# A transformer block on one Trainium2 core: the order of VectorE's work in the attention loop, the bank of two maxima a unit, and the place of one q/k set

## The chip, the core and the metric

The kernel runs on one core of one Trainium2 chip. TensorE (PE) multiplies, VectorE (DVE) and ScalarE (ACT) work on the sums in PSUM and on data in SBUF, GpSimd (POOL) on data in SBUF, and SyncE (SP) issues all DMAs here. The metric is the device time of one execution in microseconds; a lower one is better.

## The reference

Input x has 2048 tokens of 640 values. With xn = layernorm(x) the output is

```
q, k, v = split(xn @ wqkv)                 # 32 heads of 20 values
s = q k^T / sqrt(20), masked to 0 <= i - j < 256
attention = softmax(s) v @ wo
mlp = (gelu(xn @ w_gate) * (xn @ w_up)) @ w_down    # 1728 wide, gelu by tanh
out = x + attention + mlp
```

All is float32. The kernel gets the accuracy by splitting each float32 operand of the large products into a high and a low part and adding three products (high by high, low by high, high by low).

## The kernel before, in words

**Stages.** First a prologue: layernorm, transposes of x into its high and low parts `xh` and `xl`, and the first projections. Then the attention loop (`attention`, L705), which also computes most of the q, k and v projections and the first gate/up tiles of the MLP as fill. Then the other gate/up tiles (L825), and last the product with w_down and wo (L1276). The change lies in the attention loop.

**The loop.** Heads are taken in 8 groups of four and tokens in 4 chunks of 512, which makes 32 units `u = (g, c)`. A unit has 14 slots (`NS`). In each slot the program first emits the deferred work that is due (`tick`, L697), then, in even slots, two score pieces (`exp_piece`, L479: matmuls into the PSUM tile `ps_e`, L493, and an Exp on ScalarE into `P`, L495) and two or three maximum pieces, and last some 3 matmuls of fill (`pull_fill`, L700). In slot 0 it also emits the products P times V of the unit before (`av_unit`, L507: `ps_o`, L515, copied out by ScalarE into `ob`, L519), and in slot 11 the DMA loads of the q and k stacks of the unit three ahead (`load_stack`, L413, L421). A ramp of 12 slots ahead of unit 0 runs 24 maximum pieces, so the maxima run one and a half units ahead of the score pieces.

**Maxima.** The softmax needs a maximum for each row of scores. `max_piece` (L427) lets TensorE compute a 128-row strip of scores into the PSUM tile `ps_m` (L441), from a pool of three buffers (`psm`), and VectorE takes its maximum under the mask (L443, shown in the trace as the instruction itself and a short read of the accumulator `mx`). A unit has 16 of them: two in each even slot, three in slots 6 and 12. After the sixteenth, VectorE writes the negated maxima in two short instructions (L448, L449), four slots later TensorE transposes them (`max_end`, L452: `ps_n`, L455, in the same pool), ScalarE copies them to `mr` (L457) and a DMA puts them beside q in `qs` (L458), where the score pieces of that unit read them.

**Fill.** The generator `filler` (L594) yields groups of 15 matmuls with 512 columns into `ps_d` (L100, a pool of two buffers), about five slots for each group. What has to be done with a group's sum is deferred by slots with `defer` (L194):

- a q/k group (`save_qk`, L216): one slot later ScalarE copies the high part (`pt`, L235) and VectorE subtracts it (`r`, L236), one slot after that ScalarE copies the middle part (L223), POOL makes the low part (L224) and SP stores the three (L230). `r` has one buffer, `pt` two.
- a gate group and an up group (`gate_up_fill`, L550): ScalarE copies and squares (L558, L559), a slot later VectorE (L564), a slot later ScalarE's Tanh (L568), a slot later VectorE (L572), and when the up group is there VectorE multiplies (L579) and SP stores (L580).

The fill goes by the list `sets` (L589): each q/k set projects one 128-row tile of q and one of k for all four chunks, each gate/up set one tile of the MLP. The v projection of the second half of the heads (`V1_SLOT`) comes in at the first end of a chunk from slot 158 on. A stack load needs the q/k tiles of its heads in DRAM: units 24 and later need the fourth set.

**What sets the order.** On TensorE, VectorE and ScalarE the loop's instructions run in the order in which the program emits them (`manual_schedule`, L744). POOL's and SP's orders are made by the scheduler of the framework. Each engine runs its own instructions in order, so a waiting one holds all behind it. In the pages, SPq, DVEq and so on are an engine's sequencer. POOL also works in the background on sums of x (`x_sums`, L631: `tx`, L642, stored to `td`, L645), on the causal edges of `P` (L501, L504) and on the low parts of weights (L545).

Of the kernel before, what the change touches and what calls it, by code (L numbers as in the profile page):

```python
# [9 lines left out]
F32 = mybir.dt.float32  # L10
# [3 lines left out]
OP = mybir.AluOpType  # L14
# [10 lines left out]
NF = 14  # L25
# [8 lines left out]
NFA = 6  # L34
# [26 lines left out]
def block_kernel(ctx, tc, x, wqk, wv, wgu, wdo, wdl, out):  # L61
    nc = tc.nc
# [66 lines left out]
    psm = pp.enter_context(tc.tile_pool(name="psm", bufs=3, space=PSUM))  # L129
    pso = pp.enter_context(tc.tile_pool(name="pso", bufs=1, space=PSUM))  # L130
# [56 lines left out]
    acts = {}  # L187
    done = set()
    now = [None]

    def at(slot, fn, *a):
        acts.setdefault(slot, []).append((fn, a))

    def defer(n, fn, *a):  # L194
        if now[0] is None:
            fn(*a)
        else:
            at(now[0] + n, fn, *a)
# [17 lines left out]
    def save_qk(t, c, ps):  # L216
        pt = qkp.tile([128, 3, C], BF, name="pt", tag="pt")
        r = qkp.tile([128, C], F32, name="r", tag="r", bufs=1)
        dst = (qd if t < 5 else kd)[c]
        h, l = (2, 0) if t < 5 else (0, 2)  # L220

        def lower():
            nc.scalar.activation(pt[:, 1, :], r, AF.Copy)  # L223
            nc.gpsimd.tensor_tensor(out=pt[:, l, :], in0=r, in1=pt[:, 1, :], op=OP.subtract)  # L224
            a, end = t % 5 * 128, t % 5 * 128 + 128
            while a < end:
                g, b = divmod(a, 4 * DH)
                n = min(4 * DH - b, end - a)
                p = n - end + a + 128
                nc.sync.dma_start(dst[g, :, b:b + n, :].rearrange("p m t -> m p t"), pt[p - n:p])  # L230
                a += n
            done.add((t, c))

        def upper():
            nc.scalar.activation(pt[:, h, :], ps, AF.Copy)  # L235
            nc.vector.tensor_tensor(out=r, in0=ps, in1=pt[:, h, :], op=OP.subtract)  # L236
            defer(1, lower)

        defer(1, upper)

# [52 lines left out]
    def run(*gens):  # L293
        for gen in gens:
            for _ in gen:
                pass
# [84 lines left out]
    with tc.tile_pool(name="lp", bufs=1, side="right") as lp:  # L381
# [3 lines left out]
        ps = psd.tile([128, C], F32, name="ps_u", tag="dn")  # L385
# [38 lines left out]

    maxes = {}

    def max_piece(u, i):  # L427
        g, c = divmod(u, NC)
        j, b = divmod(i, 4)
        q, k = qs[u % NQ], ks[u % NK]  # L430
        if i == 0:
            maxes[u] = ap.tile([128, 4, 4], F32, name="mx", tag="mx")
        ps = psm.tile([128, 384], F32, name="ps_m", tag="mx")
        lh = q[0:120, j, 128 * b:128 * b + 128]
        old = max(0, 256 - 128 * b) if c else 0
        n0 = max(0, 128 * b - 256)
        n = old + 128 * b + 128 - n0
        parts = [(0, old, ks[(u - 1) % NK][0:120, j, C - old:C])] if old else []
        parts.append((old, n, k[0:120, j, n0:128 * b + 128]))
        for lo, hi, rhs in sorted(parts, key=lambda p: p[1] - p[0]):  # L440
            nc.tensor.matmul(ps[:, lo:hi], lh, rhs, start=True, stop=True)  # L441
        junk = ap.tile([128, 384], BF, name="junk", tag="junk", bufs=1)
        nc.vector.tensor_tensor_reduce(out=junk[:, 0:n], in0=ps[:, 0:n], in1=mask[:, 384 - n:384], scale=1.0,  # L443
                                       scalar=NEG, op0=OP.add, op1=OP.max, accum_out=maxes[u][:, j, b:b + 1])
        if i == 15:
            mx = maxes.pop(u)
            nm = nms[u % 2]
            nc.vector.tensor_scalar(nm[:, 0, 0], mx, -1.0, None, op0=OP.mult)  # L448
            nc.vector.scalar_tensor_tensor(nm[:, 0, 1], mx, -1.0, nm[:, 0, 0], op0=OP.mult, op1=OP.subtract)  # L449
            maxes[u] = nm  # L450

    def max_end(u):  # L452
        nm = maxes.pop(u)
        ps = psm.tile([128, 128], F32, name="ps_n", tag="mx")
        nc.tensor.matmul(ps, nm.rearrange("p z a j b -> p (z a j b)"), identb, start=True, stop=True)  # L455
        mr = ap.tile([32, 128], BF, name="mr", tag="mr")
        nc.scalar.activation(mr, ps[0:32], AF.Copy)  # L457
        nc.sync.dma_start(qs[u % NQ][120:122].rearrange("p j t -> p (j t)"), mr)  # L458
# [91 lines left out]
    def gate_up_fill(f, ws, c):  # L550
        cs = slice(c * C, (c + 1) * C)
        pss = []
        st = {}

        def c1():
            gs = st["g"] = hp.tile([128, C], F32, name="gs", tag="gs")
            t = st["t"] = hp.tile([128, C], F32, name="he", tag="he", bufs=2)
            nc.scalar.activation(gs, pss[0], AF.Copy)  # L558
            nc.scalar.activation(t, pss[0], AF.Square, scale=math.sqrt(0.044715))  # L559
            defer(1, c2)  # L560

        def c2():
            gs, t = st["g"], st["t"]
            nc.vector.scalar_tensor_tensor(t, t, 1.0, gs, op0=OP.add, op1=OP.mult)  # L564
            defer(1, c3)

        def c3():
            nc.scalar.activation(st["t"], st["t"], AF.Tanh, scale=math.sqrt(2.0 / math.pi))  # L568
            defer(1, c4)

        def c4():
            nc.vector.scalar_tensor_tensor(st["g"], st["t"], 1.0, st["g"], op0=OP.add, op1=OP.mult)  # L572
            st["done"] = True

        def c5():
            if "done" not in st:
                defer(1, c5)
                return
            nc.vector.scalar_tensor_tensor(st["t"], st["g"], 0.5, pss[1], op0=OP.mult, op1=OP.mult)  # L579
            nc.sync.dma_start(hd[f][c], st["t"])  # L580

        for i, (wh, wl) in enumerate(ws):
            ps = psd.tile([128, C], F32, name="ps_d", tag="dn")
            pss.append(ps)
            yield from dense_steps(ps, lambda k: wh[:, k, :], lambda k: wl[:, k, :],
                                   lambda k: xh[:, k, cs], lambda k: xl[:, k, cs], KT)
            defer(1, c5 if i else c1)

    sets = [("qk", 1), ("gu", 0), ("qk", 2), ("qk", 3), ("gu", 1), ("qk", 4)]  # L589
    sets += [("gu", f) for f in range(2, NFA)] + [("gu", NF - 1)]  # L590
    pools = (wp, None), (hp, 2)
    rest = []

# [91 lines left out]
    fill = filler()  # L685
    debt = [0.0]

    def pull_max(n, slot):
        for _ in range(n):
            x = next(stream, None)  # L690
            if x is None:
                return
            max_piece(*x)
            if x[1] == 15:
                at(slot + MXD, max_end, x[0])

    def tick():  # L697
        return [y for t in sorted(t for t in acts if t <= now[0]) for y in acts.pop(t)]

    def pull_fill(n):  # L700
        debt[0] += n
        while debt[0] > 0:
            debt[0] -= next(fill, 1.0)

    def attention():  # L705
        now[0] = -1
        load_stack(0)
        load_stack(1)
        load_stack(2)
        for i, (p, k, half) in enumerate((p, k, half) for p in range(NC // 2) for k in range(2) for half in range(2)):  # L710
            for j, fn in enumerate(x_sums(p, k, half)):
                at(XS0 + XSN * i + 2 * j, fn)
        for i in range(12):
            now[0] = i - 13
            for fn, a in tick():
                fn(*a)
            for _ in range(2):
                pull_max(1, now[0])
                pull_fill(RAMP)
        pull_fill(GAP)  # L720
        for u in range(NU + 1):
            for i in range(NS):
                T = now[0] = NS * u + i
                for fn, a in tick():
                    fn(*a)
                if i == 0 and u:
                    av_unit(u - 1)
                if i % 2 == 0:
                    if u < NU and i < 12:
                        exp_piece(u, i)  # L730
                        exp_piece(u, i + 1)
                    pull_max(3 if i in (6, 12) else 2, T)
                if i == 11 and 3 <= u + 3 < NU:
                    load_stack(u + 3)
                pull_fill(RATE / NS)
        while acts:
            now[0] += 1
            for fn, a in tick():
                fn(*a)
        now[0] = None  # L740
        run(fill)
        assert not acts
# [9 lines left out]
    c2 = c2s.enter_context(tc.tile_pool(name="c2", bufs=1, reuse_waits="tile"))  # L752
# [501 lines left out]
    late = list(tasks)[2:]  # L1254
# [21 lines left out]
    for n, (p, k) in enumerate(steps):  # L1276
        i = n % (NQD + 1)
        if i == 0:
            begun.clear()
            ps = {b: psn.tile([128, C], F32, name=f"ps_{b}", tag=f"b{b}") for b in (1, 2, 5, 3, 6, 4, 7, 8)}  # L1280
# [59 lines left out]
```

## Time and profile before

| | us |
|---|---|
| median of 3 runs | 1093.71 |
| lowest and highest | 1092.64, 1094.08 |
| the profiled execution, its own time | 1093.39 |
| its span, first to last instruction | 1091.7 |
| prologue and ramp, about | 0 to 93 |
| attention loop, about | 93 to 657 |
| other gate/up tiles, about | 657 to 835 |
| product with w_down and wo, about | 835 to 1092 |

The profiled execution takes 1.69 us beside its span. The granted TensorE clock is 0.998 of full speed over the span. A group row of the profile gives the line, the engine, the operation, the tiles (out<-in), the shape and the count, then the busy time and the mean duration in ns, then the idle time of the engine just before these instructions and what ended it. A row of waits gives the total, the number and the longest. A row of the chain gives start, length and what ran. In a timeline row the bracket is the idle time before the instruction and what ended it.

### The profile page before, as it was taken

The numbers are of one execution on the slowest core, as the hardware profiler recorded it, in microseconds if no ns is written. First come the engines' busy times: TensorE is split into PE (matmuls) and PEld (weight loads), VectorE is DVE, ScalarE is ACT, GpSimd is POOL, SyncE is SP. The second block draws the span as 40 slices with busy tenths as digits, with TensorE's granted clock in tenths as the row PEclk, the third lists the DMA queues.
The fourth block names the chain that finished last, engine by engine and source line by source line (L and its number), as shares of the span: only waits on it lengthen the run. The fifth ranks groups of instructions, "written<-read, shape, count | busy, mean of one in ns | idle before, by whom it ended". The sixth has DMA issues, their size and how long they took to land.

```text
span 1091.7 us, 20910 instructions
## 1 busy us (share of the span) xinstructions
PE 1073.2 (98%) x7253; PEld 857.9 (79%) x7253; DVE 757.4 (69%) x2089; ACT 509.7 (47%) x1031; POOL 335.3 (31%) x513
## 2 busy tenths in 40 slices
PE   8999999999999999999999999999999999999998
PEld 7887666666678766666766678888888899999998
DVE  7756667565666575666766636788875579888886
ACT  4434655465645556455555464323234453333332
POOL 5045634566726444645335240111110000000000
PEclk9999999999999999999999999999999999999999
DMA  5642343446442333353332325588764885343433
GB/s 206 195 137 82 114 143 91 132 126 181 141 135 69 87 114 112 117 163 111 103 113 83 100 62 194 178 271 286 265 210 150 293 283 166 110 141 112 138 121 114
DMA packets 96057, 162.30 MB, mean 149 GB/s; under 512 B 13248, under 2 KB 57920, under 8 KB 95952
## 3 DMA queue, kind: packets, MB, share of 16 engines
q1 hardware_dynamic: 95952, 160.97, 46.8%
q8 instruction: 57, 0.93, 0.4%
q14 instruction: 48, 0.39, 0.1%
HBM read 104.40 MB, written 56.23 MB: 147 GB/s over the span
## 4 chain that ended last, share of the span: by engine, by line
PE 78%; DVE 9%; DMA 5%; ACT 3%; issue 3%; SPq 1%; POOL 1%; DVEq 0%; ACTq 0%
PE ps_d L100 23%; PE ps_g L843 15%; PE ps L1087 12%; PE ps_o L515 7%; PE ps_e L493 7%; PE ps_m L441 6%; PE ps_v L100 6%; DVE ss L933 2%; DMA hr<-hd 1%; PE ps_g L100 1%; DVE junk L443 1%; DMA stg<-wdo 1%; DVE xr L1101 1%; ACT at L1047 1%; ACT P L495 1%
## 5 line engine op out<-in xcount | busy, mean ns | idle before, releaser
L443 DVE CUSTOM_DVE_ANT_0 junk<-ps_m,mask 128x384 bf16<-128x384 f32 (+2 forms) x512 | 271.6, 531 | 177.5 <-PE ps_m L441 136.3
L495 ACT ACTIVATE P<-ps_e 128x512 f32<-128x512 f32 (+2 forms) x384 | 197.7, 568 | 63.7 <-PE ps_e L493 57.6
L1087 PE MATMUL ps<-wb,at 128*128 128x320 f32 x999 | 159.1, 312 | 0.6 <-DVE wb L933 0.3
L1087 PEld LDWEIGHTS ps<-wb,at 128*128 128x128 f32 x999 | 150.2, 189 | 2.8 <-DVE wb L933 1.1
L501 POOL TENSOR_SCALAR_AFFINE_SELECT P<-P 128x512 f32<-128x512 f32 x128 | 84.1, 657 | 176.1 <-ACT P L495 169.1
L100 PE MATMUL ps_d<-xh,wql 128*128 128x512 f32 x430 | 129.3, 410 | 0.0
L100 PE MATMUL ps_d<-xl,wqh 128*128 128x512 f32 x430 | 128.5, 408 | 0.0
L100 PE MATMUL ps_d<-xh,wqh 128*128 128x512 f32 x430 | 128.5, 409 | 0.0
L441 PE MATMUL ps_m<-ks,qs 120*128 120x128 bf16 (+1 forms) x704 | 120.9, 275 | 3.8 <-DVE mx L443 2.0
L493 PE MATMUL ps_e<-qs,ks 122*128 122x128 bf16 (+2 forms) x704 | 113.1, 277 | 1.5 <-ACT P L495 0.8
L493 PEld LDWEIGHTS <-ks 122*128 122x128 bf16 x704 | 50.2, 98 | 55.1 <-issue 44.5
L1087 PE MATMUL ps<-wt,at 128*128 128x320 f32 x552 | 89.9, 310 | 1.2 <-DVE u L933 1.1
L100 PEld LDWEIGHTS ps_d<-xh,wql 128*128 128x128 f32 x430 | 77.9, 189 | 15.8 <-issue 2.3
L100 PEld LDWEIGHTS ps_d<-xl,wqh 128*128 128x128 f32 x430 | 78.3, 188 | 14.8 <-issue 0.6
L100 PEld LDWEIGHTS ps_d<-xh,wqh 128*128 128x128 f32 x430 | 77.7, 189 | 14.1 <-ACT xh L184 0.3
L441 PEld LDWEIGHTS <-qs 120*128 120x128 bf16 x704 | 62.1, 98 | 32.9 <-issue 14.1
L1087 PEld LDWEIGHTS ps<-wt,at 128*128 128x128 f32 x552 | 83.0, 188 | 2.3 <-DVE u L933 1.6
L515 PE MATMUL ps_o<-P,v 128*32 128x384 f32 (+2 forms) x1408 | 84.3, 386 | 0.0
L504 POOL TENSOR_SCALAR_AFFINE_SELECT P<-P 128x512 f32<-128x512 f32 x112 | 72.6, 659 | 37.4 <-ACT P L495 37.4
L224 POOL TENSOR_TENSOR pt<-r,pt 128x512 bf16<-128x512 f32 x40 | 46.8, 1170 | 79.7 <-ACT pt L223 79.6
L515 PEld LDWEIGHTS ps_o<-P,v 128*32 128x32 f32 x1408 | 40.1, 110 | 39.5 <-issue 29.2
L1047 ACT ACTIVATE at<-ss 128x512 fp32r<-128x512 f32 x59 | 37.2, 630 | 71.5 <-DVE ss L933 71.1
(179 smaller groups left out, 1696.7 us busy)
## 6 DMA issues: line engine op xcount, KB each, us to landing
hr<-hd SPq DMA_DIRECT2D x104, 128.0 KB
hd<-he SPq DMA_DIRECT2D x50, 256.0 KB
wr<-wgu SPq DMA_DIRECT2D x27, 320.0 KB
qs<-qd SPq DMA_DIRECT2D x32, 240.0 KB
ks<-kd SPq DMA_DIRECT2D x32, 240.0 KB
ats<-wdo SPq DMA_DIRECT2D x9, 640.0 KB
wtd<-ats SPq DMA_DIRECT2D x9, 640.0 KB
stg<-wtd SPq DMA_DIRECT2D x9, 640.0 KB
```

What stands on the lines that cost most here:

```text
L100: nc.tensor.matmul(ps, a(k), b(k), start=n == 0, stop=n == 3 * nk - 1)
L224: nc.gpsimd.tensor_tensor(out=pt[:, l, :], in0=r, in1=pt[:, 1, :], op=OP.subtract)
L441: nc.tensor.matmul(ps[:, lo:hi], lh, rhs, start=True, stop=True)
L443: nc.vector.tensor_tensor_reduce(out=junk[:, 0:n], in0=ps[:, 0:n], in1=mask[:, 384 - n:384], scale=1.0, scalar=NEG, op0=OP.add, op1=OP.max ...
L493: nc.tensor.matmul(ps[:, col:col + n], k[0:QROWS, j, kc:kc + 128], q[0:QROWS, j, q0:q0 + n], start=True, stop=True)
L495: nc.scalar.activation(pt[:, j, lo:hi], ps[:, lo:hi], AF.Exp, scale=SCALE)
L501: nc.gpsimd.affine_select(out=a, in_=a, pattern=[[0, 4], [1, 128]], compare_op=OP.is_ge, fill=0.0, base=0, channel_multiplier=-1)
L504: nc.gpsimd.affine_select(out=a, in_=a, pattern=[[0, 4], [-1, 128]], compare_op=OP.is_ge, fill=0.0, base=-1, channel_multiplier=1)
L515: nc.tensor.matmul(o[32 * j:32 * j + 32, q0:q0 + n], v[:, w0_:w0_ + 32], pt[:, j, col:col + n], start=i == 0, stop=i == len(todo) - 1, ski ...
L843: nc.tensor.matmul(ps, i, j, start=first and n == 0, stop=n == len(work) - 1, skip_group_check=True)
L1047: nc.scalar.activation(hi[:, 3:7], s, AF.Copy)
L1087: nc.tensor.matmul(ps[bank][:, 0:HD], a, b, start=bank not in begun, stop=final[p, bank] == n and j == len(work[bank]) - 1, skip_group_che ...
```

## The change

Three things are changed, all in the emission of the attention loop.

- **Late work.** A list `lates` takes VectorE work that is called with `late`; `flush` emits it at the end of each slot, after the slot's maxima and ahead of its fill. The subtract of a q/k group, the gate/up steps `c2`, `c4` and `c5`, and the two negations of the maxima go through it. What follows the subtract (`lower`) and what follows `c2` (`c3`) is deferred by two slots in place of one. `tick` emits `max_end` after the other deferred work of the slot.
- **Bank.** The second maximum of slot 6 and the first of slot 10 take a tile of the pool `pso`, the one bank in which `ps_o` lies, in place of one of `psm`. These are 61 of the 512 maxima.
- **Order of the fill.** In `sets` the fourth q/k set stands ahead of gate/up tile 1 instead of behind it.

No instruction is added or removed on any engine, and TensorE's instructions stand in the same order as before but for the two sets, whose matmuls have the same shapes.

```
+    lates = []
+
+    def late(fn, *a):
+        if now[0] is None:
+            fn(*a)
+        else:
+            lates.append((fn, a))
+
+    def flush():
+        while lates:
+            fn, a = lates.pop(0)
+            fn(*a)
...
+        def middle():
+            nc.vector.tensor_tensor(out=r, in0=ps, in1=pt[:, h, :], op=OP.subtract)
+            defer(2, lower)
+
         def upper():
             nc.scalar.activation(pt[:, h, :], ps, AF.Copy)
-            nc.vector.tensor_tensor(out=r, in0=ps, in1=pt[:, h, :], op=OP.subtract)
-            defer(1, lower)
+            late(middle)
...
-    def max_piece(u, i):
+    def max_piece(u, i, where):
...
-        ps = psm.tile([128, 384], F32, name="ps_m", tag="mx")
+        pool, tag = where
+        ps = pool.tile([128, 384], F32, name="ps_m", tag=tag)
...
-            nc.vector.tensor_scalar(nm[:, 0, 0], mx, -1.0, None, op0=OP.mult)
-            nc.vector.scalar_tensor_tensor(nm[:, 0, 1], mx, -1.0, nm[:, 0, 0], op0=OP.mult, op1=OP.subtract)
             maxes[u] = nm
+
+            def negate():
+                nc.vector.tensor_scalar(nm[:, 0, 0], mx, -1.0, None, op0=OP.mult)
+                nc.vector.scalar_tensor_tensor(nm[:, 0, 1], mx, -1.0, nm[:, 0, 0], op0=OP.mult, op1=OP.subtract)
+
+            late(negate)
...
-            defer(1, c2)
+            defer(1, late, c2)
...
-            defer(1, c3)
+            defer(2, c3)
...
-            defer(1, c4)
+            defer(1, late, c4)
...
-                defer(1, c5)
+                defer(1, late, c5)
...
-            defer(1, c5 if i else c1)
+            defer(1, *((late, c5) if i else (c1,)))
-
-    sets = [("qk", 1), ("gu", 0), ("qk", 2), ("qk", 3), ("gu", 1), ("qk", 4)]
-    sets += [("gu", f) for f in range(2, NFA)] + [("gu", NF - 1)]
+
+    sets = [("qk", 1), ("gu", 0), ("qk", 2), ("qk", 3), ("qk", 4)]
+    sets += [("gu", f) for f in range(1, NFA)] + [("gu", NF - 1)]
...
-    def pull_max(n, slot):
-        for _ in range(n):
+    def pull_max(n, slot, other=None):
+        for k in range(n):
...
-            max_piece(*x)
+            max_piece(*x, (pso, "o") if k == other else (psm, "mx"))
...
     def tick():
-        return [y for t in sorted(t for t in acts if t <= now[0]) for y in acts.pop(t)]
+        todo = [y for t in sorted(t for t in acts if t <= now[0]) for y in acts.pop(t)]
+        return sorted(todo, key=lambda y: y[0] is max_end)
...
                 pull_max(1, now[0])
+                flush()
                 pull_fill(RAMP)
...
-                    pull_max(3 if i in (6, 12) else 2, T)
+                    pull_max(3 if i in (6, 12) else 2, T, {6: 1, 10: 0}.get(i))
+                flush()
                 if i == 11 and 3 <= u + 3 < NU:
                     load_stack(u + 3)
                 pull_fill(RATE / NS)
...
             for fn, a in tick():
                 fn(*a)
+            flush()
```

## The prediction on record

> **What bounds the kernel now.** I read the page's busy line first, then the table by stretches for the attention loop, then TensorE's groups in that stretch.
>
> ```profile
> PE 1073.2 (98%) x7253; PEld 857.9 (79%) x7253; DVE 757.4 (69%) x2089; ACT 509.7 (47%) x1031; POOL 335.3 (31%) x513
> 93.00:657.00 564.00, 558.52 (x4256) 391.16 (x4254) 355.20 (x1175) 310.09 (x642) 286.19 (x453) 1.00 0.38 114
> L441 PE MATMUL ps_m<-ks,qs 120*128 120x384 bf16 (+2 forms) x672 | 113.0, 275 | 3.8 <-DVE mx L443 2.0 <-DMA sd<-ob 1.5
> L493 PE MATMUL ps_e<-qs,ks 122*128 122x256 bf16 (+2 forms) x702 | 112.6, 277 | 1.5 <-ACT P L495 0.8
> ```
>
> TensorE bounds the loop: busy 558.52 of 564.00 us, with VectorE at 355.20 and ScalarE at 310.09. The change gives TensorE the same matmuls in the same order, so all it can win in the loop is TensorE's waiting. The visible part is 564.00 - 558.52 = 5.48 us, nearly all of it ahead of the maxima (3.8) and the score pieces (1.5). As the ends of matmuls are modelled, a short wait can hide under the matmul before, so this is a low figure. A better one comes from the lengths of the units. Each unit begins with the products P times V, so the starts of `ps_o` in the chain that ended last mark the units (the x32 rows are unit 1 and every fourth after it; they follow a first chunk, which has fewer pieces).
>
> ```profile
> 106.12 2.08 PE ps_o L515 x32
> ...
> 285.49 2.73 PE ps_o L515 x48
> 303.04 2.73 PE ps_o L515 x48
> ...
> 373.51 2.73 PE ps_o L515 x48
> 390.90 2.08 PE ps_o L515 x32
> 408.22 2.73 PE ps_o L515 x48
> 425.87 2.73 PE ps_o L515 x48
> 443.66 2.77 PE ps_o L515 x48
> 480.74 2.73 PE ps_o L515 x48
> ...
> 622.77 2.73 PE ps_o L515 x48
> ```
>
> Units 1 to 29 take 622.77 - 106.12 = 516.65 us, 17.82 each, or 17.82 / 14 = 1.27 a slot. A good unit of each chunk: unit 16 takes 390.90 - 373.51 = 17.39, unit 17 takes 17.32, unit 18 takes 17.65, unit 11 takes 303.04 - 285.49 = 17.55, together 69.91. Seven such fours and one more unit like 17 make 7 x 69.91 + 17.32 = 506.69. So about **10.0 us** of the loop is irregular waiting, and the change can win that and little more.
>
> What these waits are is seen in timelines. First VectorE and then TensorE in unit 1, slots 10 to 12:
>
> ```profile
> 118.04 0.56 DVE L443 CUSTOM_DVE_ANT_0 junk<-ps_m,mask 128x384 bf16<-128x384 f32 x1
> ...
> 118.75 0.56 DVE L443 CUSTOM_DVE_ANT_0 junk<-ps_m,mask 128x384 bf16<-128x384 f32 x1
> ...
> 120.21 0.69 DVE L236 TENSOR_TENSOR r<-ps_d,pt 128x512 f32<-128x512 f32 x1 [0.89 <-ACT pt L235]
> 120.81 0.55 DVE L443 CUSTOM_DVE_ANT_0 junk<-ps_m,mask 128x384 bf16<-128x384 f32 x1
> ```
>
> ```profile
> 122.48 0.32 PE L441 MATMUL ps_m<-ks,qs 120*128 120x384 bf16 x1 [0.65 <-DVE mx L443]
> ```
>
> The subtract stands ahead of the slot's maxima and waits 0.89 us for ScalarE's copy; the maxima wait behind it, their buffers stay full, and TensorE stands 0.65 us. A maximum takes 118.75 - 118.04 = 0.71 us with its readout. Second, ScalarE in unit 9, and its waits for VectorE over the loop:
>
> ```profile
> 255.34 0.60 ACT L235 ACTIVATE pt<-ps_d 128x512 bf16<-128x512 f32 x1
> 256.76 0.63 ACT L223 ACTIVATE pt<-r 128x512 bf16<-128x512 f32 x1 [0.83 <-DVE r L236]
> 257.30 2.14 ACT L495 ACTIVATE P<-ps_e 128x512 f32<-128x512 f32 x4
> ```
>
> ```profile
> ACT he L568 <- DVE he L564: 15.1, 13, 2.2
> ...
> ACT pt L223 <- DVE r L236: 13.8, 18, 1.9
> ```
>
> With one slot between the subtract and the copy that needs it, ScalarE reaches the copy too early and stands (13 + 18 times), and then does four Exps in a row: the score pieces behind find their two buffers full. Third, SyncE and TensorE in units 20 and 21:
>
> ```profile
> 451.75 7.11 SPq L645 DMA_DIRECT2D td<-tx  x2
> ...
> 464.20 0.78 SPq L230 DMA_DIRECT2D kd<-pt  x2
> 465.07 1.37 SPq L421 DMA_DIRECT2D qs<-qd  x3
> 466.49 1.10 SPq L421 DMA_DIRECT2D ks<-kd  x3
> ```
>
> ```profile
> 472.73 0.33 PE L441 MATMUL ps_m<-ks,qs 120*128 120x128 bf16 x2 [1.50 <-DMA sd<-ob]
> ```
>
> SP holds at a store of `tx`, then at the last store of the fourth q/k set (`kd`); only then come the stack loads of unit 23, and TensorE waits 1.50 us for them at its first maximum of that unit. Units 20 and 21 together take 480.74 - 443.66 = 37.08, against 17.39 + 17.32 = 34.71 for their kind.
>
> **The change part by part.** No instruction comes or goes, so every term is a wait.
>
> *Late work.* The waits other than the one of the stack are 10.0 - 1.5 = 8.5 us; they come from VectorE's order and from ScalarE waiting for VectorE. With the maxima first, the subtract's wait for ScalarE lies beside 2 x 0.71 = 1.42 us of maxima, more than the 0.89 seen. Its own end moves back: in a slot with two maxima it ends 1.42 + 0.69 = 2.11 us after the first maximum begins, in one with three 3 x 0.71 + 0.69 = 2.82. What needs it now comes two slots later, 2 x 1.27 = 2.54. So in six of seven slots (all but slots 6 and 12) ScalarE finds it done, in the others it waits some 0.3 us. The negations, 0.53 us for the second one, go behind the third maximum of slot 6 too:
>
> ```profile
> L449 DVE SCALAR_TENSOR_TENSOR nm<-mx,nm 128x16 bf16<-128x16 f32 x31 | 16.5, 533 | 1.1
> ```
>
> Behind the late work stand only the next even slot's maxima, which start two slots later anyway. `ps_d` is kept some 1.4 us longer; its buffer is next wanted a whole group (five slots, 6.3 us) later, so this costs nothing, and without that cover up to 1.4 a group. The sum of one unit of 16 x 0.71 = 11.4 us of maxima and about three groups' late work of 0.7 to 2.1 fits in 17.4. Of the 8.5 us I take four fifths, **-6.8**: below it is nothing (the waits only change place), above it all 8.5.
>
> *Bank.* 61 of the 512 maxima get a fourth buffer. The one of slot 6 waits for ScalarE's copy of `ps_o`, issued in slot 0; that of slot 10 must be read before `ps_o` is written again, four slots or 5.1 us later, against 0.71. Nothing waits there. Alone it gains where a slot with three maxima meets a late VectorE, which is in the 8.5 already: 0 here. If VectorE were late by more than four slots, P times V would stand, by as much.
>
> *Order of the fill.* The fourth set's 120 matmuls, its eight sums with their copies, subtracts and POOL parts, its 16 stores, its two loads and its splits move ahead of gate/up tile 1's 120 matmuls, ScalarE and VectorE steps, four stores and two loads; on SP and POOL they change places with these. TensorE's sum is the same. At the time of the stack of unit 23 SP then has no `kd` store in front of it and POOL no low part of a set, so the 1.50 us go: **-1.5**, bounded by 0 (the `tx` store still stands ahead) and -2.4 (37.08 - 34.71). What was at that place now falls some three units earlier, on other stacks, which is in the next term.
>
> *New waits.* ScalarE still meets slots with three maxima, stores come a slot later, and `mr` is emitted behind the slot's other ScalarE work. I take **+0.5**, between 0 and the rivals below.
>
> *A rule of the Trainium skill.* VectorE's two steps with both inputs in SBUF now lie elsewhere beside POOL's work:
>
> ```profile
> L564 DVE SCALAR_TENSOR_TENSOR he<-he,gs x24: 685/691/1169, 148.8 to 652.0; 128x512 f32<-128x512 f32 x24
> L572 DVE SCALAR_TENSOR_TENSOR gs<-he,gs x24: 679/687/1089, 150.6 to 653.5; 128x512 f32<-128x512 f32 x24
> ```
>
> A few take 0.4 to 0.48 us more than the median. The Trainium skill (SBUF — State Buffer, section Who interferes with whom) says why: a VectorE instruction with two SBUF inputs and a GpSimd one that reads SBUF exclude each other for a whole instruction. The long ones in these rows agree. By that rule alone the loss is that of the third rival.
>
> **Sum.** -6.8 - 1.5 + 0.5 = -7.8. The profiled execution's own time is 1093.39 (span 1091.7 and 1.69 around it): 1093.39 - 7.8 = **1085.6 us**, 0.74% under the median 1093.71, which lies 0.3 above the profiled execution. With all of the 10.0 and 0.4 of unit 0 it would be 1083.0. The stages after the loop follow it at a fixed distance.
>
> **The rivals.**
>
> 1. *Half comes back.* In slots with three maxima, or where ScalarE runs late, the late step still misses its user. Half of the 6.8 stays, and SP finds the stack of unit 23 late as before: -3.4 + 0.5 = -2.9, 1090.5 us. For it: 31 waits of ScalarE are to be cured by one more slot, and VectorE's part moves back by up to three maxima (2.1 us), more than that slot (1.27). Against it: six of seven slots have room.
> 2. *Slower: SP's queue.* SP already stands at stores whose data is not ready:
>
> ```profile
> SPq L580 <- DVE he L579: 71.3, 17, 8.5
> SPq L230 <- POOL pt L224: 68.8, 25, 5.5
> ```
>
>    Both kinds become ready later (by up to 2.1 us and by 1.27), and stack loads and `mr` queue behind. The rows of the copy, of its DMA's issue, and of a small store from issue to landing in the chain:
>
> ```profile
> L457 ACT ACTIVATE mr<-ps_n x32: 250/268/268, 85.8 to 636.2; 32x128 bf16<-32x128 f32 x32
> ```
>
> ```profile
> L458 SPq DMA_DIRECT2D qs<-mr x32: 632/667/712, 86.1 to 636.7; - x32
> ```
>
> ```profile
> 591.89 1.71 DMA sd<-ob
> ```
>
>    `mr` leaves TensorE in slot 10 and is needed in slot 14, 5.1 us later; less 0.27 for the copy, 0.67 for the issue and, as an estimate from the store, 1.7 for landing, 2.4 are free. Where SP is held longer than that, TensorE waits. If eight of the units lost 1.5 us each, as unit 21 does now, that is +12.0 - 6.8 + 0.5 = +5.7: 1099.1 us. Against it: the profile shows one such wait in 31 units.
> 3. *Same: POOL and VectorE in each other's way.* If all 48 of the steps above took 0.45 more, one in a slot with three maxima would end 2.13 + 1.15 = 3.28 us after the first, 0.7 beyond the two slots. At 0.15 us of TensorE for each that is 7.2, and the gain is gone: 1085.6 + 7.2 = 1092.8. The medians, at the lowest value, speak against it.
>
> That the change does not do what it says is hardly possible: VectorE's order is written out by hand.
>
> **How the numbers follow.** Forecast (1083.0 to 1088.5): 0.60. Half comes back (1088.5 to 1091.5): 0.18. No change (1091.5 to 1095.9): 0.10, half of it the third rival and half waits that only change their place. SP's queue, slower than 1095.9: 0.09. Better than 1083.0: 0.03. A measurement of this kernel can tell 0.2% (2.2 us) from no change, which gives faster 0.60 + 0.18 + 0.03 = 0.81, same 0.10, slower 0.09. The range 1083.0 to 1092.0 leaves out 0.03, 0.09 and most of the 0.10, about 0.2.
>
> **What would show it.** Late work: TensorE's idle time ahead of the maxima falls from 3.8 us to under 1, ScalarE's waits of 15.1 and 13.8 to a third, and units 1 to 29 take some 509 us. Order of the fill: no stand of TensorE at the first maximum of unit 23. Wrong would be: idle time ahead of the score pieces above 1.5 us, with SP held at a store just before; a wait of P times V for a maximum; or units that keep their 17.8 us.

## The result and the profile after

The changed kernel takes **1096.7 us** (median of 8 runs, 1093.79 to 1099.39), the kernel before in the same series 1093.89 (8 runs, 1091.78 to 1095.58). The ratio is 1.0026 with a 95% interval of 1.0014 to 1.0039: slower by about 2.8 us, where the prediction said 8 us faster. The profiled execution of the changed kernel took 1098.06 us, 4.67 more than that of the kernel before (1093.39), so part of what follows is larger in it than in the median.

The line numbers move: L441, L443, L493, L515 of the kernel before are L458, L460, L514, L536 after; the subtract L236 is L248, the copies L235 and L223 are L252 and L236, POOL's L224 is L237, the store of `mr` L458 is L479, the stores of `pt` and `tx` L230 and L645 are L243 and L666. The split of the weights in the ramp is L92 in both.

First TensorE's groups of the kernel after from 93 to 662 us, the loop, as they were shown of before:

```profile
L458 PE MATMUL ps_m<-ks,qs 120*128 120x384 bf16 (+2 forms) x676 | 113.3, 275 | 1.1 <-DVE mx L460 0.7
L514 PE MATMUL ps_e<-qs,ks 122*128 122x128 bf16 (+2 forms) x704 | 112.9, 278 | 3.8 <-DMA qs<-mr 3.6
L100 PE MATMUL ps_v<-wvh,xh 128*128 128x320 f32 x97 | 20.0, 322 | 1.4 <-DVE v L305 1.4
```

TensorE's idle time ahead of the maxima fell from 3.8 to 1.1 us, as forecast. But ahead of the score pieces it rose from 1.5 to 3.8, nearly all of it a wait for `mr`, and a v projection now waits 1.4 us for VectorE.

Where the time went is read from the starts of `ps_o` in the chain. One row of the kernel before that was not shown, then three of the kernel after:

```profile
124.18 2.73 PE ps_o L515 x48
```

```profile
128.98 2.73 PE ps_o L536 x48
...
310.34 2.73 PE ps_o L536 x48
...
628.06 2.73 PE ps_o L536 x48
```

Unit 2 begins at 128.98 instead of 124.18: 4.80 us are lost before it. Units 2 to 29 take 628.06 - 128.98 = 499.08 against 622.77 - 124.18 = 498.59: +0.49. What follows takes 0.62 less (1098.06 - 628.06 = 470.00 against 470.62). 4.80 + 0.49 - 0.62 = 4.67. So the loop as a whole gained nothing, and what lies ahead of it lost.

Two of these figures are not the change's alone. Of the 4.80 us, 1.89 are there before the ramp's stands: a subtract well ahead of them (L236, then L248) begins at 61.72 instead of 59.83. Most of that comes from a stretch at half clock, told below. And the 0.62 less at the end hides that only the kernel before has such a stretch there (at 860.83, shown in the last section). Within the loop the 0.49 is a loss and a gain: units 2 to 11 take 310.34 - 128.98 = 181.36 against 303.04 - 124.18 = 178.86, 2.50 more, and units 12 to 29 take 317.72 against 319.73, 2.01 less. The loss lies at the start of unit 10.

**The ramp.** The two stands of TensorE there, which the kernel before does not have:

```profile
76.19 0.41 PE L100 MATMUL ps_v<-wvh,xh 128*128 128x320 f32 x1 [1.86 <-DVE r L248]
...
95.93 0.97 PE L100 MATMUL ps_v<-wvh,xh 128*128 128x320 f32 x5 [1.24 <-DVE v L305]
```

The matmul ahead of each began 2.17 and 1.55 us earlier, where 0.15 is usual: the two cost 2.0 and 1.4 us. VectorE and ScalarE around the first, in the kernel after:

```profile
75.45 0.69 DVE L248 TENSOR_TENSOR r<-ps_d,pt 128x512 f32<-128x512 f32 x1 [2.58 <-POOL pt L237]
```

```profile
71.91 0.74 ACT L92 ACTIVATE wqh<-wr 128x640 fp32r<-128x640 f32 x1 [2.79 <-PE ps_d L100]
72.56 0.61 ACT L236 ACTIVATE pt<-r 128x512 bf16<-128x512 f32 x1
```

and ScalarE in the kernel before:

```profile
67.43 0.63 ACT L223 ACTIVATE pt<-r 128x512 bf16<-128x512 f32 x1 [0.83 <-DVE r L236]
67.97 0.72 ACT L92 ACTIVATE wqh<-wr 128x640 fp32r<-128x640 f32 x1
70.02 0.74 ACT L92 ACTIVATE wqh<-wr 128x640 fp32r<-128x640 f32 x1 [1.33 <-PE ps_d L100]
```

The reader is to follow the one buffer `r`. Deferred by two slots, its copy (L236) now stands behind both halves of the weights' split, the second of which waits 2.79 us for TensorE. So POOL gives `r` back late (its L237 ends at 75.42, by its timeline), the next subtract waits 2.58 us for it, and with the subtract `ps_d`, one of the two buffers in which the v groups that follow also lie.

**The start of unit 10.** SyncE, first after, then before:

```profile
270.96 0.32 SPq L666 DMA_DIRECT2D td<-tx  x1
271.37 2.37 SPq L243 DMA_DIRECT2D qd<-pt  x3
273.83 0.66 SPq L479 DMA_DIRECT2D qs<-mr  x1
```

```profile
264.37 1.31 SPq L230 DMA_DIRECT2D qd<-pt  x3
...
267.10 0.34 SPq L645 DMA_DIRECT2D td<-tx  x1
267.53 0.66 SPq L458 DMA_DIRECT2D qs<-mr  x1
```

and in the kernel after ScalarE's copy and the first score piece of unit 10:

```profile
266.90 0.25 ACT L478 ACTIVATE mr<-ps_n 32x128 bf16<-32x128 f32 x1
```

```profile
275.84 0.60 PE L514 MATMUL ps_e<-qs,ks 122*128 122x128 bf16 x4 [3.01 <-DMA qs<-mr]
```

`mr` lies ready from 267.15 on, but SP holds at the store of `tx` until 270.96, and the three stores of `qd`, which went ahead of `tx` before, now stand between `tx` and `mr`. TensorE waits 3.01 us. This is the second rival's mechanism, in one unit.

**The clock.** The table by stretches, at that place:

```profile
273.70:277.11 3.41, 1.27 (x11) 1.03 (x11) 0.47 (x1) 0.85 (x2) 3.33 (x8) 1.00 0.65 203
277.12:280.52 3.40, 3.40 (x12) 2.19 (x11) 0.99 (x5) 1.83 (x5) 2.34 (x3) 0.50 0.79 220
280.53:283.94 3.41, 3.41 (x20) 2.39 (x19) 2.61 (x9) 2.55 (x5) 2.70 (x5) 1.00 0.69 215
```

A row gives the stretch and its length, then the busy time and the count of PE, PEld, DVE, ACT and POOL; the third number from the end is the granted clock. Behind the stand TensorE runs for 3.4 us at half clock and does 12 matmuls where the next stretch does 20: about 1.7 us more. A second such stretch lies from 14.29 to 17.70 us, in the prologue, which the change leaves as it was and where the kernel before has none in its profile. Of the kernels below e5, e6 and e10 have one there and the others don't, so it is not put down to the change.

### The profile page after: what moved, and what is told of

It is laid out like the page before. It is cut to its first block, busy times and chain, and to the rows that moved or that the text cites. A ratio compares the mean times of both kernels' runs of the same rounds, so it can differ in the third digit from the quotient of the medians.

```text
span 1096.4 us, 20897 instructions
## 1 busy us (share of the span) xinstructions
PE 1074.1 (98%) x7253; PEld 859.0 (78%) x7253; DVE 757.9 (69%) x2089; ACT 508.8 (46%) x1031; POOL 340.1 (31%) x513
## 4 chain that ended last, share of the span: by engine, by line
PE 76%; DVE 6%; DMA 4%; ACT 2%; POOL 2%; issue 2%; SPq 1%; DVEq 0%; ACTq 0%; POOLq 0%
PE ps_d L100 23%; PE ps_g L868 15%; PE ps L1112 13%; PE ps_e L514 7%; PE ps_o L536 7%; PE ps_m L458 6%; PE ps_v L100 4%; DVE junk L460 1%; PE ps_g L100 1%; DMA hr<-od 1%; DMA hr<-hd 1%; DMA stg<-wdo 1%; DVE ss L958 1%; POOL tx L663 1%; DVE xr L1126 1%
## 5 line engine op out<-in xcount | busy, mean ns | idle before, releaser
L460 DVE CUSTOM_DVE_ANT_0 junk<-ps_m,mask 128x384 bf16<-128x384 f32 (+2 forms) x512 | 272.2, 532 | 188.1 <-PE ps_m L458 143.1
L522 POOL TENSOR_SCALAR_AFFINE_SELECT P<-P 128x512 f32<-128x512 f32 x128 | 86.3, 674 | 169.2 <-ACT P L516 167.0
L458 PE MATMUL ps_m<-ks,qs 120*128 120x128 bf16 (+1 forms) x704 | 120.7, 276 | 1.1 <-DVE mx L460 0.7
L514 PE MATMUL ps_e<-qs,ks 122*128 122x128 bf16 (+2 forms) x704 | 112.9, 278 | 3.8 <-DMA qs<-mr 3.6
L514 PEld LDWEIGHTS <-ks 122*128 122x128 bf16 x704 | 50.3, 98 | 56.9 <-issue 45.5
L458 PEld LDWEIGHTS <-qs 120*128 120x128 bf16 x704 | 62.2, 98 | 29.5 <-issue 11.9
L536 PE MATMUL ps_o<-P,v 128*32 128x384 f32 (+2 forms) x1408 | 84.3, 386 | 0.0
L525 POOL TENSOR_SCALAR_AFFINE_SELECT P<-P 128x512 f32<-128x512 f32 x112 | 72.6, 659 | 33.6 <-ACT P L516 33.6
L237 POOL TENSOR_TENSOR pt<-r,pt 128x512 bf16<-128x512 f32 x40 | 46.8, 1170 | 88.2 <-ACT pt L236 88.2
L536 PEld LDWEIGHTS ps_o<-P,v 128*32 128x32 f32 x1408 | 40.1, 110 | 39.5 <-issue 30.0
```

Source lines behind the costliest of these rows:

```text
L514: nc.tensor.matmul(ps[:, col:col + n], k[0:QROWS, j, kc:kc + 128], q[0:QROWS, j, q0:q0 + n], start=True, stop=True)
L522: nc.gpsimd.affine_select(out=a, in_=a, pattern=[[0, 4], [1, 128]], compare_op=OP.is_ge, fill=0.0, base=0, channel_multiplier=-1)
L525: nc.gpsimd.affine_select(out=a, in_=a, pattern=[[0, 4], [-1, 128]], compare_op=OP.is_ge, fill=0.0, base=-1, channel_multiplier=1)
L536: nc.tensor.matmul(o[32 * j:32 * j + 32, q0:q0 + n], v[:, w0_:w0_ + 32], pt[:, j, col:col + n], start=i == 0, stop=i == len(todo) - 1, ski ...
```

## The experiments

Two theories were to be told apart. **Theory:** the new order does cure waits in the loop, but in the ramp the late subtract and the copy deferred by two slots cost 3.4 us, and the new order on SP costs 3 to 5 us in one unit. **Rival:** the bank or the moved set is what costs. All ratios are to the kernel before on the same chip (its medians there were 1094.04 us for e1 to e4, 1092.90 for e5 to e8 and 1094.04 for e9 to e12); the column of times is not to be compared across these groups. The expectations name the stand of `mr` by the products just ahead of it, those of unit 9; it is the start of unit 10. Their units 11, 19 and 27 are likewise 12, 20 and 28 here.

| kernel | us | ratio, 95% interval |
|---|---|---|
| changed | 1096.70 | 1.0026, 1.0014 to 1.0039 |
| e1, ramp at once | 1092.90 | 0.9983, 0.9972 to 0.9994 |
| e2, `mr` in turn | 1096.14 | 1.0016, 1.0004 to 1.0028 |
| e3, sets back | 1095.87 | 1.0010, 0.9999 to 1.0020 |
| e4, no bank | 1098.73 | 1.0045, 1.0028 to 1.0062 |
| e5, ramp at once, `mr` first | 1090.18 | 0.9974, 0.9963 to 0.9985 |
| e6, before with the bank alone | 1091.21 | 0.9984, 0.9971 to 0.9997 |
| e7, before with the set alone | 1092.35 | 0.9996, 0.9984 to 1.0008 |
| e8, late work alone | 1099.22 | 1.0058, 1.0038 to 1.0079 |
| e9, ramp with one slot | 1095.04 | 1.0004, 0.9987 to 1.0020 |
| e10, as e8 with both cures of e5 | 1091.79 | 0.9983, 0.9972 to 0.9993 |
| e11, as e5 with sets back | 1090.63 | 0.9965, 0.9953 to 0.9978 |
| e12, as e5 with a third maximum in the bank | 1090.84 | 0.9972, 0.9962 to 0.9982 |

**The ramp, e1 and e9.**

```
     def late(fn, *a):
-        if now[0] is None:
+        if now[0] is None or now[0] < 1:
             fn(*a)
...
-            defer(2, lower)
+            defer(1 if now[0] is not None and now[0] < 1 else 2, lower)
```

> The changed kernel, but ahead of the loop's slot 1 the late work is done at once and the copy of `r` one slot later, as in the kernel before; in the loop all stays late. Theory: the late subtract costs the ramp 2.0 us at 74 us and 1.4 us at 94 us, since `r` is one buffer and `ps_d` two and groups follow each other in under two slots there. Both stands go: 1096.7 - 3.4 = 1093.3 us, P times V of unit 1 starts 3.4 us earlier. Rival (the ramp's stands are only brought forward from a wait that comes anyway, or the loss sits in the bank or in the moved set): 1096.7 within 1.

Measured: 0.9983, some 0.4% under the changed kernel. Both stands of the ramp are gone from TensorE's timeline, and the changed kernel without this one fault is faster than the kernel before. The rival that the stands are only brought forward falls; the bank and the moved set are answered by e4 and e3 below.

e9 has the second half of this edit alone (the `defer` of `lower`).

> The changed kernel with one edit: ahead of slot 1 the copy of `r` comes one slot after the subtract, as before; the subtract itself stays late there. VectorE's order is that of the changed kernel. Theory: the 2.0 us stand at 74 us is the copy's, which stood behind the second half of the weights' split and held the one buffer of `r`; it goes. The 1.4 us stand at 94 us is the subtract's, which comes behind the sums of the filler's next group, and stays. 1096.7 - 2.0 = 1094.7 us. Rival (both stands come from the late subtract): both stay, 1096.7 within 0.7.

Measured: 1.0004, which is the 1094.7 us forecast within its interval, and of the two stands one is left. TensorE between 60 and 100 us in e9:

```profile
91.26 0.97 PE L100 MATMUL ps_v<-wvh,xh 128*128 128x320 f32 x5 [1.24 <-DVE v L305]
```

So the stand at 74 us is the copy's, which held `r`, and the one at 94 us is the late subtract's. VectorE in the changed kernel there:

```profile
95.54 0.24 DVE L305 COPY v<-ps_v 128x80 f32<-128x80 f32 x1 [0.30 <-ACT v L307]
...
98.64 0.69 DVE L248 TENSOR_TENSOR r<-ps_d,pt 128x512 f32<-128x512 f32 x1
```

The subtract of the ramp's last q/k group now comes at 98.64, behind slot 0's maxima; the next v group began at 95.93, right after the copies of the v group ahead of it. One of the two `ps_d` buffers is held by the subtract, and the v groups share the other: so the rows are read here. A second buffer for `r` was not tried.

**SP's queue, e2 and e5.** e2 emits a slot's steps in the order in which they were entered, e5 puts `max_end` first and has the ramp of e1.

```
-        return sorted(todo, key=lambda y: y[0] is max_end)
+        return todo                                              # e2
+        return sorted(todo, key=lambda y: y[0] is not max_end)   # e5
```

> The changed kernel, but a slot's steps are emitted in the order in which they were entered, as before: `mr` no longer goes behind the slot's other steps. Theory: in unit 9 SP held `mr` behind three stores of `qd` (2.37 us of issue) that stood ahead of it because of the new order; `mr` goes ahead of them, TensorE's 3.0 us stand falls to about 0.6, and the 3.4 us stretch at half clock that follows it, worth 1.7, goes with it: 1096.7 - 2.4 - 1.7 = 1092.6 us. Rival (the stand is set by the store of `tx` ahead, whose data come late from GpSimd, and not by the order of `mr`): `mr` still waits, the stand stays above 2 us, 1096.7 within 1.

Measured: 1.0016, less than forecast, and by the times alone not told from the changed kernel. The trace shows why: TensorE's groups in e2 and then in e5, over the loop.

```profile
L458 PE MATMUL ps_m<-ks,qs 120*128 120x384 bf16 (+2 forms) x676 | 113.0, 275 | 1.8 <-DVE mx L460 0.6 <-DMA od<-ob 0.6
L514 PE MATMUL ps_e<-qs,ks 122*128 122x128 bf16 (+2 forms) x704 | 112.6, 277 | 1.8 <-ACT P L516 1.0 <-DMA qs<-mr 0.5
```

```profile
L458 PE MATMUL ps_m<-ks,qs 120*128 120x384 bf16 (+2 forms) x676 | 113.0, 275 | 1.7 <-DMA od<-ob 0.6 <-DVE mx L460 0.6
L514 PE MATMUL ps_e<-qs,ks 122*128 122x128 bf16 (+2 forms) x704 | 112.8, 277 | 0.7 <-ACT P L516 0.4
```

In e2 the wait for `mr` fell from 3.6 to 0.5 us; a wait for the stack load behind it on SP (0.6, `od<-ob`) and one for ScalarE in the same unit (1.0) took a part of its place. The half clock of unit 10 is gone too, as expected, but the ramp's two stands are there.

> The changed kernel with the ramp's late work done at once (as in e1_ramp_at_once) and `mr` ahead of the slot's other steps instead of behind them; in unit 9 its store then stands ahead of the store of `tx` on SP. Theory: the stand of 3.4 us in unit 9 of e1_ramp_at_once goes; as in e2_mr_in_turn up to 1.9 of it comes back as waits for the stack load and the Exps of that unit. 1092.9 - 3.4 + 1 = 1090.5 us (1089.5 to 1091.5). Rival (the stand only changes its name: the stack load behind the same stores is late by as much): 1092.9 within 0.7.

Measured: 0.9974, within the range forecast. SP in e5 at the same place:

```profile
261.95 0.66 SPq L479 DMA_DIRECT2D qs<-mr  x1
266.74 0.32 SPq L666 DMA_DIRECT2D td<-tx  x1
267.15 2.04 SPq L243 DMA_DIRECT2D qd<-pt  x3
```

`mr` leaves 4.8 us ahead of the store of `tx`, and no score piece waits for it. Against e1 the gain is 0.1% by the times, with intervals that overlap: that the stand goes is shown by the trace, its worth in the median (0 to 3 us) is not settled. In the two traces units 1 to 29 take 513.04 us in e5 and 514.84 in e1, 1.80 less.

**The bank, e4 and e6.** e4 is the changed kernel with `pull_max(..., T)` as before, e6 the kernel before with the bank's lines alone.

```
-                    pull_max(3 if i in (6, 12) else 2, T, {6: 1, 10: 0}.get(i))
+                    pull_max(3 if i in (6, 12) else 2, T)        # e4
```

> The changed kernel without the fourth buffer: all maxima of a unit use the three buffers they had. Theory: the bank only adds room; without it the third maximum of slots 6 and 12 waits a little longer for VectorE, 0 to 1 us over the loop: 1097.2 us. Rival (the bank makes P times V or the maxima wait, which is the loss): 1094 us or less, and fewer waits ahead of P times V.

> The kernel before with the bank alone: the second maximum of slot 6 and the first of slot 10 use the buffer of the P times V sums. By the prediction, nothing: 1094.0 us. By e4_no_bank, where the bank's loss added 3 us of waits ahead of maxima, it takes waits out by itself, 1 to 2.5 us of the 6.6 ahead of maxima: 1092.3 us. Rival (it helps only where the maxima come first, and here ties P times V to VectorE's order): 1094.5 or more.

Measured: without the bank 1.0045, with the bank alone 0.9984. By these the bank is worth 1.7 us alone and 2.1 beside the rest of the change, and twice the rival is wrong. The first is clear of noise (0.3 to 3.2 us), the second by itself is not (2.1 with some 2.3 either way). A third pair, e3 and e8, which also differ by the bank alone, gives 5.2 with some 2.5 either way. The maxima in e4 and in e6:

```profile
L458 PE MATMUL ps_m<-ks,qs 120*128 120x384 bf16 (+2 forms) x676 | 113.4, 275 | 3.1 <-DVE mx L460 2.7
```

```profile
L442 PE MATMUL ps_m<-ks,qs 120*128 120x384 bf16 (+2 forms) x672 | 111.7, 275 | 3.5 <-DMA od<-ob 1.7 <-DVE mx L444 1.4
```

In e4 VectorE's part of the wait is 2.7 against 0.7 with the bank; in e6 it is 1.4 against 2.0 in the kernel before, and the 1.7 left over is the stack of unit 23.

**The set, e3, e7 and e11.**

```
-    sets = [("qk", 1), ("gu", 0), ("qk", 2), ("qk", 3), ("qk", 4)]
-    sets += [("gu", f) for f in range(1, NFA)] + [("gu", NF - 1)]
+    sets = [("qk", 1), ("gu", 0), ("qk", 2), ("qk", 3), ("gu", 1), ("qk", 4)]
+    sets += [("gu", f) for f in range(2, NFA)] + [("gu", NF - 1)]
```

> The changed kernel with the sets of the fill in the order of the kernel before (fourth q/k set behind gate/up tile 1). Theory: the move of the set cures the wait of 1.5 us for the stack of unit 23 and costs nothing else, so undone it gives 1096.7 + 1.5 = 1098.2 us, with TensorE standing at the first maximum of unit 23. Rival (the moved set is what makes the changed kernel slower): 1094 us or less.

> The kernel before with the fourth q/k set ahead of gate/up tile 1 and nothing else. By the prediction TensorE's wait for the stack of unit 23 goes: 1094.0 - 1.5 = 1092.5 us. By e3_sets_back, where the order of before came out no slower, the moved set costs elsewhere what it gains there: 1094 within 1, with another wait in its place.

> As e5_ramp_mr_first (late work at once in the ramp, `mr` first, bank), with the sets of the kernel before. Theory: the moved set gains nothing, since e3_sets_back showed no stand at the stack of unit 23 with the sets of before: the time of e5_ramp_mr_first within 1, 1090.8 us beside a kernel before of 1093.5. By the prediction: 1.5 more, 1092.3 us, and a stand at the first maximum of unit 23.

Measured: the move alone gives 0.9996, no difference. Undone in the changed kernel it gives 1.0010, undone in e5 0.9965: no loss in either, rather a gain of 0.1 to 0.16% within the intervals. The fourth pair that differs by the set alone, e4 and e8, goes the other way by 0.13%, within the intervals too. So together the four show no gain. In e3 TensorE does not stand at the stack of unit 23 any more, though the set lies where it lay before: with the late order that stand is not there. Another of about its size lies near that place, in TensorE's timeline of e3:

```profile
469.92 0.64 PE L536 MATMUL ps_o<-P,v 128*32 128x256 f32 x8 [1.41 <-POOL P L522]
```

And in e7, where the stand at the stack is gone by the move, others grew: TensorE's two groups in e7 over the loop.

```profile
L493 PE MATMUL ps_e<-qs,ks 122*128 122x256 bf16 (+2 forms) x702 | 112.9, 277 | 2.2 <-ACT P L495 1.4
L441 PE MATMUL ps_m<-ks,qs 120*128 120x384 bf16 (+2 forms) x672 | 112.6, 275 | 2.7 <-DVE mx L443 2.4
```

The waits for the stack (1.5) went, those for VectorE rose from 2.0 to 2.4 and those for ScalarE from 0.8 to 1.4. e11, the changed kernel with both cures and without the moved set, has the lowest ratio of the study: 0.35% under the kernel before, 0.6% under the changed one. e5 and e12 lie within its interval.

**The late work, e8 and e10.** e8 is the changed kernel without bank and moved set (the two edits above), e10 the same with the ramp and the `mr` of e5.

> The changed kernel without the bank and with the sets in the order of before: the late work alone, with `mr` last in its slot. By the prediction's terms -6.8 + 0.5: 1087.7 us. Theory by now: the ramp's 3.4, unit 9's 3 and its half clock of 1.7 against 3 to 4 us cured in the loop, and waits of maxima left without the bank: 1097.9 us (1096.5 to 1099).

> The late work alone without its two side effects: sets and buffers of the kernel before, the late work in the loop, at once in the ramp, and `mr` first in its slot. The prediction's term for it is -6.8 us (1086.7 beside a kernel before of 1093.5). Theory by now: e5_ramp_mr_first gained 2.7 with bank and sets, the bank alone gained 1.7, the sets nothing that can be told, so the late work is worth 1 us and not 6.8: 1092.5 us (1091.5 to 1094). Rival (bank and late work cure the same waits): 1091 us or less.

Measured: 1.0058, a little above the theory's range, and 0.9983, within it. The late work as it was written costs over half a percent when nothing else is there, and without its two side effects it gains 1.9 us, where the prediction had 6.8. The rival (bank and late work cure the same) is not borne out by the medians: 1.7 of the bank and 1.9 of the late work are 3.6, against the 3.8 of e11. With intervals of over 1 us on each, it is not ruled out in part: in the traces units 1 to 29 are 1.75 shorter in e6, 1.24 in e10, and 2.32 in e11. What kept the late work small is seen in e10, over the loop:

```profile
L458 PE MATMUL ps_m<-ks,qs 120*128 120x384 bf16 (+2 forms) x672 | 112.7, 275 | 3.7 <-DVE mx L460 3.4
L514 PE MATMUL ps_e<-qs,ks 122*128 122x256 bf16 (+2 forms) x702 | 112.1, 277 | 0.5
```

Ahead of the score pieces the wait fell from 1.5 to 0.5; ahead of the maxima VectorE's part rose, from 2.0 to 3.4. VectorE in e10, behind slot 6 of a unit:

```profile
597.90 0.69 DVE L593 SCALAR_TENSOR_TENSOR gs<-he,gs 128x512 f32<-128x512 f32 x1
598.50 0.61 DVE L468 TENSOR_SCALAR nm<-mx 128x16 bf16<-128x16 f32 x1
599.15 0.40 DVE L469 SCALAR_TENSOR_TENSOR nm<-mx,nm 128x16 bf16<-128x16 f32 x1
599.47 0.67 DVE L600 SCALAR_TENSOR_TENSOR he<-gs,ps_d 128x512 f32<-128x512 f32 x1
600.07 0.55 DVE L460 CUSTOM_DVE_ANT_0 junk<-ps_m,mask 128x384 bf16<-128x384 f32 x1
```

```profile
600.67 0.32 PE L458 MATMUL ps_m<-ks,qs 120*128 120x384 bf16 x1 [0.62 <-DVE mx L460]
601.38 0.33 PE L458 MATMUL ps_m<-ks,qs 120*128 120x128 bf16 x2 [0.39 <-DVE mx L460]
```

Four late steps in a row, 597.90 to 600.07, stand ahead of the next slot's maxima, and TensorE waits for these instead. The bank takes most of that away: in e11 VectorE's part over the loop is 0.5 us, 0.45 of it at this place.

**A third maximum in the bank, e12.**

```
-                    pull_max(3 if i in (6, 12) else 2, T, {6: 1, 10: 0}.get(i))
+                    pull_max(3 if i in (6, 12) else 2, T, {6: 1, 8: 0, 10: 0}.get(i))
```

> As e5_ramp_mr_first, and the first maximum of slot 8 uses the buffer of the P times V sums too. Theory: the stands left ahead of maxima in slot 8 (0.3 in unit 19, 0.6 in unit 27, 0.3 in unit 11) shrink: 0.5 to 1 us under e5_ramp_mr_first, 1090.1 us beside a kernel before of 1093.5. Rival (the one buffer is asked for in three slots running, and the next maximum waits for the one before): no gain, or 1091 us and more.

Measured: 0.9972 beside 0.9974 of e5: no difference, since VectorE's part of the waits there is 0.8 us as against 0.6.

## Why the prediction was wrong

The forecast was -7.8 us, the measurement +2.8. The largest error is the late-work term, which promised some 5 us too much. That the kernel became slower comes from two costs, in the ramp and at `mr`, which the prediction put at nothing and too low; without the ramp's alone (e1) it is already faster than the kernel before. With both cured (e5) the change gains 2.8 us, which is still not the forecast.

- **`ps_d` "costs nothing": the step that failed outright.** "Its buffer is next wanted a whole group (five slots, 6.3 us) later" holds in the loop and not in the ramp, where a group of 15 matmuls takes some two slots and a v group little more than one. The one buffer `r`, which the two-slot delay holds longer, has no term at all. The prediction named the price if that cover is gone ("up to 1.4 a group") and did not ask where it is gone. e1 and e9 show it: 2.0 us by the copy that held `r`, 1.4 by the subtract; undone, the ratio falls from 1.0026 to 0.9983, 4.7 us, with 1.2 to 1.4 us of uncertainty in either.
- **New waits, +0.5: mis-sized.** That stores come later and `mr` behind the slot's other work was seen, and the mechanism was the second rival's; it was priced as eight units of 1.5 us and given 0.09. It came in one unit with 3.0 us, and the half clock behind it added 1.7 in the profiled execution. SP held `mr` for 273.83 - 267.15 = 6.68 us and TensorE waited 3.01, so 3.7 us were free, and not 2.4. Already in the kernel before SP held it there for 267.53 - 263.25 = 4.3 us (the copy ends at 263.25), and TensorE did not stand. e2 and e5 show that the order does it.
- **Late work, -6.8: mis-sized.** e10 gives 1.9. Units 1 to 29, of which some 509 us were forecast, take 516.65 before, 515.41 in e10 and 513.04 in e5, the lowest of the traces. So most of the 8.5 us of waits did not go (or were never there to be had, which no run settles): "behind the late work stand only the next even slot's maxima, which start two slots later anyway" fails where late steps heap up. And ScalarE's waits, of which a third was to be left, grew instead. In the kernel after, from 93 to 662 us:

```profile
ACT pt L236 <- DVE r L248: 25.7, 21, 3.0
ACT he L589 <- DVE he L585: 15.4, 13, 2.7
```

  Against 13.8 and 15.1 before. Yet the score pieces wait less for ScalarE (0.5 us in all in e10): the three longest of these waits (2.98, 2.68 and 2.63 us) fall where no score piece is due, in slots 12 and 13 and under the P times V that follow. They were the wrong witness: what counts is TensorE's idle time, not ScalarE's.
- **Bank, 0: mis-sized.** It gains 1.7 us by itself (e6) and 2.1 beside the late work (e4). "Which is in the 8.5 already" may be right as to where the waits are; it was wrong as to which edit cures them.
- **Order of the fill, -1.5: not borne out.** The stand went as forecast, but e7 gives -0.4 us with 1.3 either way (its interval just reaches -1.7), and the two pairs with e3 and e11 leave no room for 1.5, as waits for VectorE and ScalarE came elsewhere; and with the late order the stand is not there anyway (e3). "What was at that place now falls some three units earlier" was said and priced with nothing.
- **What held:** TensorE's idle time ahead of the maxima fell to 1.1 us ("under 1"), no stand at the first maximum of unit 23, the stages behind the loop at a fixed distance to 0.6 us, in part by luck: without the half-clock stretch that only the kernel before has there, it would be some 1.1 us more, as an estimate from 1.7 - 0.62. The third rival did not come: the medians of the two steps with both inputs in SBUF are 687 and 689 ns after, 691 and 687 before, and again only a few are long.

The sum that the runs give: late work -1.9, bank -1.7, set 0, ramp +3.4 (traces) to +4.7 (e1), `mr` +1 to +3 (e2 and e5, the trace). That makes +0.8 to +4.1, against +2.8 measured. What of it the half-clock stretches are is not settled; they differ from run to run. By the granted clocks, 0.9969 of the changed kernel against 0.9979 to 0.9984 of the kernel before in the three series, they may be 1.1 to 1.6 of the 2.8 us, as an estimate.

## What to carry to other kernels

A step that is put off costs nothing only while its buffers have slack, and that has to be asked at the tightest place, the ramp, with the number of buffers in hand, not in the steady loop. When an order is changed, look at what the in-order queues behind it (here SP's) now carry ahead of the one transfer that the next unit waits for. And a long wait of an engine that is not the bottleneck is no gain to be had: only the bottleneck's own idle time, place by place, is.

## What the runs showed of the hardware

A stand of TensorE of some 2 to 3 us can be followed by a stretch of 3.4 us at half clock. Beside unit 10 above, two cases from the tables by stretches: e8 at its first ramp stand, and e1 at its 3.3 us wait for `mr`.

```profile
72.40:75.80 3.40, 1.55 (x10) 1.38 (x11) 1.90 (x7) 0.99 (x3) 1.32 (x2) 1.00 0.39 112
75.82:79.20 3.38, 3.38 (x15) 2.98 (x14) 0.87 (x4) 0.24 (x1) 0.90 (x1) 0.50 0.46 129
```

```profile
264.73:268.13 3.40, 1.63 (x32) 0.83 (x25) 0.00 (x0) 0.60 (x1) 3.24 (x6) 1.00 0.35 99
268.14:271.54 3.40, 1.83 (x13) 1.51 (x13) 0.89 (x3) 1.42 (x3) 3.24 (x7) 1.00 0.74 216
271.56:274.96 3.40, 3.40 (x24) 2.36 (x23) 1.98 (x8) 2.60 (x7) 3.03 (x5) 1.00 0.76 193
```

The stretches are cut so that their edges fall on the steps of the clock in that trace, which lie a whole number of 3.413 us apart (in the kernel after 277.12 - 14.29 = 262.83, 77 times 3.413). In e8 a window with TensorE busy for 1.55 us was followed by half clock; in e1 the longer wait fell across two windows (1.63 and 1.83 busy) and nothing followed. So a stand of this size can cost 1.7 us more or nothing. The Trainium skill (TensorE: Matmul & The Clock Gate, Part 1) tells of a free-running window of 3413 ns and of half rate after an idle one; the length agrees with these rows, while here windows that were busy for 1.27 and 1.55 us, and so not idle, were followed by it. Over the runs the clock differs as well: over the 8 runs of the changed kernel the mean granted clock was 0.9969, over the 12 of e5 0.9983. One stretch takes 3.41 / 2 / 1096 = 0.0016 off, so the changed kernel had about 0.9 more of them a run, as an estimate. What decides it is open, and the busy time of the window alone does not. In the kernel before, a window of 1.80 us of work was followed by half clock, between those 1.63 and 1.83 that were not. In the kernel after, the one from 10.88 to 14.29 us was busy for 2.31 and was followed by half clock; in e8, the one from 273.76 to 277.17 us was busy for 1.58, with the stand for `mr` in it, and was not.

```profile
857.41:860.81 3.40, 1.80 (x10) 1.31 (x10) 2.04 (x4) 3.35 (x4) 0.00 (x0) 1.00 0.70 264
860.83:864.20 3.37, 3.37 (x14) 3.07 (x13) 3.12 (x3) 1.79 (x2) 0.00 (x0) 0.50 0.97 287
```
